# A spectral filter and an MLP mixed by a gate, in split fp32: another table of steps and another table of buffer slots

## The chip, the cores and the metric

The kernel runs on one core of one Trainium2 chip. The metric is the device time of one execution in microseconds (us); of several runs the median is taken. The engines are PE (TensorE: matmuls), PEld (its weight loads), DVE (VectorE), ACT (ScalarE), POOL (GpSimd) and SP (SyncE, which here issues DMAs).

## The reference: what is computed

The input x has 2048 rows (S) of 512 values (D), the MLP is 1792 wide (F).

```python
def _A_ref(x, w_r, w_i):
    X = rfft2(x) * (w_r + 1j * w_i)
    return irfft2(X, s=(S, D))
def _B_ref(x, w1, b1, w2, b2):
    return gelu(x @ w1 + b1) @ w2 + b2
g = sigmoid((x * gate_w).sum(-1, keepdims=True))
return g * a + (1 - g) * b
```

## The kernel before

**The work.** Branch A is the spectral filter. The two-dimensional FFT is done as matmuls with tables of cosines and sines. Per group of rows, a transform along D (`pd`, from the sums and differences eo and w that DVE builds of x) is copied to `zb` in halves and multiplied by `tf` (`py`); radix-4 butterflies over the 16 groups run on DVE (L665 to L673: b0s, b0d, y), the filter is multiplied in (m and wf, L765 to L769), and the butterflies run back. The inverse is `pz` (from the table tg, multiplied by the gate at L797, and pq), copied to `zb`, and `pa`. Of each pair of pa tiles, ACT copies one (od, L844), and DVE takes sum and difference with the other (u L854, v L855). L864 makes w of u and v, POOL adds the gate's part with an accumulating DMA (L867), and SP writes w out (L868).

Branch B is the MLP in 14 blocks of 128 of F. Per block f, `ph` holds x·W1 (512 columns wide), ACT does the gelu in place (L904), the result is split into g_fh and g_fl (ACT L466, DVE L467), and `po` (first pass, groups of rows 0 and 1) or `poB` (second pass) accumulates it times W2 over a range of blocks; the sums of ranges are put together in DRAM (`bacc`) by POOL's accumulating DMAs (L407). In the second pass a part of the x·W1 products is formed with fewer matmuls from sums of tiles (`nu`, `ux`, L1090 and on).

**The halves.** Every value is held as a high and a low half that PE takes as fp32r, and every product is three matmuls: high·high, low·high and high·low (suffixes h and l: mxh and mxl of x, wa0h and wa0l of W1's block 0, wb0h and wb0l of W2's block 0). A matmul is 128x512 unless a row says otherwise. For blocks of W2, and W1's later blocks, `halve` (L872) makes the halves: SP loads the block (L877, `..._raw`), ACT rounds it to the high half (L878), ACT writes the negative high half into the low half's tile (L472), and POOL issues a DMA that adds the block to it again (L407). W1's first blocks are loaded by SP (L890, L893; tile war) and split by ACT (L894) and DVE (L896). Block 0's and the first two groups of x come in two halves each (L503 by ACT's queue, L505 and L890 by SP's).

**What sets the order.** The kernel first records 2015 steps in a graph (`Graph.add`), each with an engine, the buffers it reads and writes, and a cost and a lag for a planner that ran beforehand. `Graph.schedule` then emits them in the order that the table ORDER (L125 to L204) gives by step numbers, and takes each buffer's slot in its pool from the table SLOTS (L206 to L225). Cost and lag are not read when the kernel is built. An engine runs its instructions in the order in which they are emitted, and waits at the first one whose inputs aren't there. So ORDER sets the queue of each engine, the DMA issues of SP, ACT and POOL among them, and SLOTS sets which earlier reader a buffer must wait for.

**The start and the end.** PE first runs fillers: six 128x512 matmuls of a zero tile and FILL = 10 of 128x256, tile `none` (L416). They keep it running until the first halves of x and W1 are there. At the end (`last`) the second pass's last poB tiles are subtracted from y on DVE (L1171) and written out by SP (L1174); of the last tile, the second 256 columns are computed apart (poB_33256), subtracted in two pieces (L1164) and written by SP and by ACT's queue (L1169).

Of the kernel before, what the change touches and what calls it, by code (L numbers as in the profile page):

```python
# [345 lines left out]
def tile_kernel(ctx: ExitStack, tc: tile.TileContext, xt, xc, w1, w2, b1, b2, x0g, wf, wrev, out, consts):  # L346
# [10 lines left out]
    vec, act, pe, sp = nc.vector, nc.scalar, nc.tensor, nc.sync  # L357
# [5 lines left out]
    add = g.add  # L363
# [517 lines left out]
    def load_w(n, f):  # L881
        first = n == "a" and f == 0
        h, l = W[n, f] = [buf("w", [P, D], F32R, f"w{n}{f}{k}", cls=n + k, parts=2 if first and k == "h" else 1) for k in "hl"]
        src = (w1 if n == "a" else w2)[f]
# [394 lines left out]
```

## Time and profile before

| | us |
|---|---|
| runs: lowest, median, highest | 365.43, 366.06, 366.5 |
| the profiled execution | 364.17 |
| its span | 362.3 |
| PE busy | 356.1 (98%) |
| DVE busy | 330.8 (91%) |
| ACT busy | 253.6 (70%) |
| POOL busy | 70.6 (19%) |
| first real matmul starts | 5.50 |
| last matmul starts | 358.23 |

The span runs from the first instruction of the profile to the last event; what the execution takes beyond it lies around it. The granted TensorE clock was full throughout. A matmul's record is longer than the distance to the next one's start, since matmuls overlap, so PE's progress is read from starts. In a row of a timeline stand the start, the duration, the engine, the line, the operation, output <- inputs, the shape and the number of instructions in the row; in brackets stands the idle time before it, and what ended it. fp32 matmuls (pd, pz) leave two records each.

### The profile page before, as it was taken

The page shows a single profiled execution, that of the slowest core. Times are in us where ns is not written, and L with a number is a line of the kernel's source. Part 1 is how long each engine was busy: PE and PEld are TensorE (multiplying, and loading weights), DVE is VectorE, ACT ScalarE, POOL GpSimd, SP SyncE. Part 2 cuts the span into 40 slices and gives each one's busy share as a digit, 9 for nine tenths or more (in the row PEclk, how much of TensorE's full clock was granted, in tenths as well). Part 3 has the DMA queues.
Part 4 walks back from the last instruction along what each step waited for, and adds up shares of the span by engine and source line. Part 5 has one row for each costly group of instructions (what it writes and reads, how often), then busy time and mean ns, then how long its engine had stood idle before and what let it go on. Part 6 is the DMA issues. An engine that isn't in the chain of part 4 may idle for free.

```text
span 362.3 us, 5722 instructions
## 1 busy us (share of the span) xinstructions
PE 356.1 (98%) x1808; PEld 302.2 (83%) x1808; DVE 330.8 (91%) x745; ACT 253.6 (70%) x471; POOL 70.6 (19%) x91
## 2 busy tenths in 40 slices
PE   8999999999999999999999999999999999999995
PEld 6988898898877888888888888888888888888885
DVE  5969999799978999999999999979989899899994
ACT  4984688789985563348468764899999986786100
POOL 1030000111021240111224300000432222003220
PEclk9999999999999999999999999999999999999999
DMA  7999597377689899897998954445686588858787
GB/s 242 369 337 263 176 322 203 102 162 184 208 147 237 199 261 211 198 342 226 217 263 152 148 113 134 103 133 166 83 146 123 85 149 208 166 164 203 168 228 221
DMA packets 46494, 70.34 MB, mean 194 GB/s; under 512 B 5376, under 2 KB 19200, under 8 KB 46464
## 3 DMA queue, kind: packets, MB, share of 16 engines
q1 hardware_dynamic: 34592, 48.93, 41.5%
q0 software_dynamic: 11440, 20.72, 37.1%
q10 hardware_dynamic: 432, 0.33, 0.3%
q8 instruction: 14, 0.23, 0.3%
q14 instruction: 16, 0.13, 0.1%
HBM read 48.32 MB, written 19.41 MB: 187 GB/s over the span
## 4 chain that ended last, share of the span: by engine, by line
PE 85%; DMA 5%; DVE 4%; ACT 3%; SPq 1%; issue 1%; DVEq 0%
PE poB L416 21%; PE po L416 20%; PE ph L416 14%; PE ux L1090 10%; PE nu L1090 8%; PE pz L416 4%; PE pd L416 3%; PE py L416 3%; PE pa L416 3%; DMA wb1l<-in_w 2%; DMA wb1l_raw<-in_w 2%; DMA y<-ownr 1%; ACT ph L904 1%; DVE b0s L665 0%; SPq L893 0%
## 5 line engine op out<-in xcount | busy, mean ns | idle before, releaser
L904 ACT ACTIVATE ph<-ph,b1t 128x512 f32<-128x512 f32 x28 | 18.4, 656 | 17.9 <-PE ph L416 17.8
L803 ACT ACTIVATE sw<-y,al 64x512 f32<-64x512 f32 x32 | 22.9, 721 | 1.2 <-DVE y L669 0.5
L407 POOL DMA_DIRECT2D bacc<-oB x16 | 13.9, 936 | 47.1 <-ACT oB L982 46.1
L407 POOL DMA_DIRECT2D bacc<-o x16 | 15.6, 977 | 35.8 <-ACT o L982 35.5
L765 DVE TENSOR_TENSOR m<-y,wf 128x514 f32<-128x514 f32 x32 | 21.3, 691 | 0.3
L982 ACT ACTIVATE o<-po 128x512 f32<-128x512 f32 x16 | 9.5, 596 | 15.4 <-PE po L416 9.9
L416 PEld LDWEIGHTS pz<-tg,pq 128*128 128x128 f32 x128 | 17.1, 191 | 1.9 <-PE pz L416 0.4
L416 PE MATMUL pz<-tg,pq 128*128 128x128 f32 x128 | 17.8, 275 | 0.3 <-DVE v L855 0.3
L416 PE MATMUL pd<-cf,w 128*128 128x129 f32 x128 | 17.7, 274 | 0.0
L1090 PE MATMUL nu<-xf,wa0h 128*128 128x512 f32 x56 | 17.4, 392 | 0.0
L416 PE MATMUL py<-zb,tf 128*128 128x258 f32 x96 | 17.3, 297 | 0.0
L416 PEld LDWEIGHTS pd<-cf,w 128*128 128x128 f32 x128 | 16.6, 190 | 0.6
L607 DVE TENSOR_TENSOR zb<-pd,zb 128x256 fp32r<-128x256 f32 x32 | 13.1, 419 | 4.1 <-ACT zb L604 2.2
L632 ACT ACTIVATE y<-pys 64x257 f32<-64x257 f32 x32 | 13.1, 417 | 3.5 <-DVE pys L629 3.0
L810 DVE SCALAR_TENSOR_TENSOR pq<-y,al,sw 128x256 f32<-128x256 f32 x32 | 14.9, 483 | 0.6 <-ACT sw L806 0.5
L416 PEld LDWEIGHTS pa<-zb,ci 128*128 128x128 f32 x96 | 13.7, 188 | 1.4
L416 PEld LDWEIGHTS py<-zb,tf 128*128 128x128 f32 x96 | 14.1, 190 | 0.9
L416 PE MATMUL pa<-zb,ci 128*128 128x256 f32 x96 | 14.3, 281 | 0.0
L822 ACT ACTIVATE zb<-pz 128x512 fp32r<-128x512 f32 x16 | 9.4, 597 | 6.5 <-PE pz L416 6.4
L604 ACT ACTIVATE zb<-pd 128x256 fp32r<-128x256 f32 x32 | 11.2, 387 | 3.5 <-PE py L416 2.2
L823 DVE TENSOR_TENSOR zb<-pz,zb 128x512 fp32r<-128x512 f32 x16 | 11.0, 691 | 2.8 <-ACT zb L822 2.8
L574 DVE TENSOR_TENSOR w<-eo 128x256 f32<-128x256 f32 x32 | 13.1, 421 | 0.3
(700 smaller groups left out, 1279.9 us busy)
## 6 DMA issues: line engine op xcount, KB each, us to landing
wf<-in_wf SPq DMA_DIRECT2D x16, 257.0 KB, 4.9
bacc<-o POOLq DMA_DIRECT2D x16, 256.0 KB, 7.0
bacc<-oB POOLq DMA_DIRECT2D x16, 256.0 KB, 4.2
xf<-in_xt SPq DMA_DIRECT2D x14, 256.0 KB, 4.9
wr<-in_w SPq DMA_DIRECT2D x14, 256.0 KB, 5.0
tf<-tf SPq DMA_DIRECT2D x16, 192.0 KB, 5.1
bacc<-o SPq DMA_DIRECT2D x8, 256.0 KB, 3.8
bacc<-oB SPq DMA_DIRECT2D x8, 256.0 KB, 2.2
```

The lines of the kernel that those rows point to most:

```text
L407: return add("pool", 2.3 * kb / 340, 3.4, lambda: nc.gpsimd.dma_start(dst(), src(), accum_op=ALU.add), reads, writes, rank)
L416: pe.matmul(ps, w, x, start=start, stop=stop)
L574: v(lambda s=s, op=op: vec.tensor_tensor(w.ap()[:, s], eo.ap()[:, :, 0], eo.ap()[:, :, 1], op=op), 256, [eo], [(w, s)], feed)
L604: a(lambda c=c: act.activation(segs(xh, c), both(c), AF.Copy), 256, [ps[c]], [(xh, c)], 0)
L607: v(lambda c=c: vec.tensor_tensor(segs(xl, c), both(c), segs(xh, c), op=ALU.subtract), 256, [ps[c], (xh, c)], [(xl, c)], 0)
L632: a(lambda o=o, i=i: act.activation(Y[j].ap()[o:o + HP, 1], pys.ap()[i:i + HP, 1], AF.Copy), 257, [(pys, 1)], [(Y[j], 1 + k)], 0, more=0.1)
L765: v(lambda mk=mk, k=k, y=y, w=w: vec.tensor_tensor(mk.ap(), y.ap(), w.ap()[:, k:k + 1, :ND].to_broadcast([P, 2, ND]), op=ALU.mult), 514, [ ...
L803: a(lambda sw=sw, y=y, o=o, i=i: act.activation(sw.ap()[o:o + HP], y.ap()[i:i + HP, ::-1, :HD], AF.Copy, scale=al.ap()[i:i + HP, 0:1]), 51 ...
L810: v(lambda sw=sw, pq_=pq_, y=y, j=j, k=k, op=op: vec.scalar_tensor_tensor(pq_.ap()[:, k], y.ap()[:, k, :HD], al.ap()[:, 1 + j:2 + j], sw.a ...
L823: v(lambda n=n, ps=ps: vec.tensor_tensor(zl.ap()[:, :, :, n], ps.ap(), zh.ap()[:, :, :, n], op=ALU.subtract), 512, [ps, (zh, n)], [(zl, n) ...
L904: a(lambda: act.activation(ps.ap(), ps.ap(), AF.Gelu_apprx_tanh, bias=b1t.ap()[:, f:f + 1]), 600, [b1t], [ps]).table = "gelu"
L1090: pe.matmul(o.ap(), w(wi, e), FX[j].ap()[:, xi, e], start=first, stop=k == 5, skip_group_check=not start)
```

## The change

The tables ORDER and SLOTS are replaced, and three of the planner's lags are changed: for the two halves of x's group 0 (L503), of group 4 (L505) and of W1's block 0 (L890). The graph is the same: the same 2015 steps with the same dependencies, so each engine runs the same instructions, in another order and with other slots. A tile's number changes with the order (zb_101 and zb_128 are zb_86 and zb_107 in the new order).

The diff has 103 replaced lines of the two tables; the first of ORDER and the last of SLOTS stand here, and all the rest:

```diff
 ORDER = """
-13 0 2 3 4 5 6 7 8 9 10 11 12 15 38 14 16 26 25 506 508 18 507 527 109 1 37 39 27 19 64 17 511 23 554 543 530 167 509
...
+0 2 15 3 22 13 1 16 23 24 38 37 508 509 14 4 5 6 7 26 27 506 507 25 527 39 65 17 18 19 64 66 543 61 511 8 9 10 109 515
...
@@ -500,9 +500,9 @@
     x4 = buf("w", [P, NQ, P], F32, "xf4", parts=2, cls="x")
     XF = {0: x0, 4: x4}
     for k in range(2):
-        add("act", 0.4, 3.0, lambda k=k: act.dma_start(x0.ap()[:, 2 * k:2 * k + 2].rearrange("p a b -> p (a b)"),
+        add("act", 0.4, 2.4 + 0.35 * k, lambda k=k: act.dma_start(x0.ap()[:, 2 * k:2 * k + 2].rearrange("p a b -> p (a b)"),
                                                        x0g[:, k * HD:(k + 1) * HD]), [], [(x0, k)], 0)
-        add("sp", 128 / 340, 2.4, lambda k=k: sp.dma_start(x4.ap()[:, 2 * k:2 * k + 2], xt[4][:, 2 * k:2 * k + 2]), [], [(x4, k)],
+        add("sp", 128 / 340, 1.5 + 0.05 * k, lambda k=k: sp.dma_start(x4.ap()[:, 2 * k:2 * k + 2], xt[4][:, 2 * k:2 * k + 2]), [], [(x4, k)],
             0.01 + 0.01 * k)
     for j in NORD[2:4]:
         XF[j] = load_x(j, "f")
@@ -887,7 +887,7 @@
         if first:
             for k in range(2):
                 o = slice(k * HD, (k + 1) * HD)
-                add("sp", 128 / 340, 1.4 + 0.2 * k, lambda o=o: sp.dma_start(t.ap()[:, o], src[:, o]), [], [(t, k)])
+                add("sp", 128 / 340, 1.0 + 0.25 * k, lambda o=o: sp.dma_start(t.ap()[:, o], src[:, o]), [], [(t, k)])
                 v(lambda o=o: vec.tensor_copy(h.ap()[:, o], t.ap()[:, o]), 256, [(t, k)], [(h, k)])
         elif own:
             dma(lambda: sp.dma_start(t.ap(), src), 256, [], [t])
```

Where the order changes, three places.

The first is ACT's queue in the first 25 us, in two cuts. ph is x·W1 before the gelu, wb the blocks of W2, L878 a high half, L472 the negative high half that POOL's accumulation waits for. Around wb1l, before:

```order
L904 ACTIVATE ph_0_160<-ph_0_160,b1t 128x512
L878 ACTIVATE wb4h<-wb4l_raw 128x512
L559 ACTIVATE mxh_240<-xf_136 128x512
L904 ACTIVATE ph_1_192<-ph_1_192,b1t 128x512
L472 ACTIVATE wb4l<-wb4h 128x512
L466 ACTIVATE g_1h<-ph_1_192 128x512
L894 ACTIVATE wa4h<-war_143 128x512
L878 ACTIVATE wb2h<-wb2l_raw 128x512
L472 ACTIVATE wb2l<-wb2h 128x512
L472 ACTIVATE wb1l<-wb1h 128x512
```

and in the new order:

```order
L878 ACTIVATE wb0h<-wb0l_raw 128x512
L472 ACTIVATE wb0l<-wb0h 128x512
L878 ACTIVATE wb1h<-wb1l_raw 128x512
L904 ACTIVATE ph_1_170<-ph_1_170,b1t 128x512
L466 ACTIVATE g_1h<-ph_1_170 128x512
L904 ACTIVATE ph_0_137<-ph_0_137,b1t 128x512
L894 ACTIVATE wa3h<-war_165 128x512
L466 ACTIVATE g_0h<-ph_0_137 128x512
L894 ACTIVATE wa4h<-war_159 128x512
L472 ACTIVATE wb1l<-wb1h 128x512
```

wb1l's L472 stood 23rd in ACT's queue, behind the two instructions each of wb4 and wb2; now it stands 19th, ahead of them. Around wb3l, before (zb are the copies of PE's pd tiles):

```order
L878 ACTIVATE wb3h<-wb3l_raw 128x512
L904 ACTIVATE ph_4_318<-ph_4_318,b1t 128x512
L466 ACTIVATE g_4h<-ph_4_318 128x512
L472 ACTIVATE wb3l<-wb3h 128x512
L604 ACTIVATE zb_101<-pd_386 128x256
L604 ACTIVATE zb_128<-pd_363 128x2x128
```

and in the new order:

```order
L466 ACTIVATE g_3h<-ph_3_268 128x512
L604 ACTIVATE zb_86<-pd_349 128x2x128
L604 ACTIVATE zb_107<-pd_353 128x2x128
L878 ACTIVATE wb3h<-wb3l_raw 128x512
L604 ACTIVATE zb_107<-pd_357 128x256
L904 ACTIVATE ph_4_302<-ph_4_302,b1t 128x512
L604 ACTIVATE zb_86<-pd_359 128x256
L472 ACTIVATE wb3l<-wb3h 128x512
```

wb3l's L472 stood 32nd, ahead of all copies of pd; now it is 35th, behind four of them and behind the gelu of block 4. POOL issues the accumulations in the order wb0l, wb1l, wb2l, wb3l, wb4l in both, so wb4l's waits behind wb3l's in both, too.

The second place is DVE's queue around g_9l, the low half of the gelu's output of block 9. b0s, b0d, y, m and wf belong to the filter. Before:

```order
L667 TENSOR_TENSOR b0d_1528<-y 128x514
L667 TENSOR_TENSOR y<-b0s_1524,b0s_1500 128x514
L665 TENSOR_TENSOR y<-b0d_1517,b0d_1528 128x2x257
L765 TENSOR_TENSOR m_8_1545<-y,wf_1344 128x514
L765 TENSOR_TENSOR m_8_1548<-y,wf_1344 128x514
L667 TENSOR_TENSOR y<-b0d_1528,b0d_1517 128x2x257
L767 TENSOR_TENSOR y<-m_8_1548,m_8_1545 128x257
L769 TENSOR_TENSOR y<-m_8_1548,m_8_1545 128x257
L665 TENSOR_TENSOR y<-b0s_1500,b0s_1524 128x514
L467 TENSOR_TENSOR g_9l<-ph_9_1502,g_9h 128x512
```

and in the new order:

```order
L665 TENSOR_TENSOR b0s_1521<-y 128x514
L665 TENSOR_TENSOR b0s_1526<-y 128x514
L667 TENSOR_TENSOR b0d_1529<-y 128x514
L667 TENSOR_TENSOR b0d_1531<-y 128x514
L665 TENSOR_TENSOR y<-b0s_1526,b0s_1521 128x514
L765 TENSOR_TENSOR m_0_1548<-y,wf_1175 128x514
L765 TENSOR_TENSOR m_0_1567<-y,wf_1175 128x514
L665 TENSOR_TENSOR y<-b0d_1531,b0d_1529 128x2x257
L467 TENSOR_TENSOR g_9l<-ph_9_1505,g_9h 128x512
L667 TENSOR_TENSOR y<-b0s_1521,b0s_1526 128x514
L467 TENSOR_TENSOR g_8l<-ph_8_1480,g_8h 128x512
```

g_9l stands behind eight instructions of the filter in place of ten. On PE, the first matmul that reads block 9's output came 24 matmuls behind the last ph of that block, and in the new order 39 matmuls behind it.

The third place is the end of SP's queue, the writes of the output. Before:

```order
L1174 DMA out<-oB_31_4142 128x512
L1174 DMA out<-oB_23_4148 128x512
L868 DMA out<-w_4085 128x2x256
L1174 DMA out<-oB_30_4160 128x512
L868 DMA out<-w_4109 128x2x256
L1174 DMA out<-oB_32_4168 128x512
L1174 DMA out<-oB_33_4187 128x256
L1169 DMA out<-oB_33_4187 128x128
```

and in the new order:

```order
L1174 DMA out<-oB_23_4126 128x512
L1174 DMA out<-oB_30_4150 128x512
L1174 DMA out<-oB_33_4166 128x256
L868 DMA out<-w_4112 128x2x256
L1174 DMA out<-oB_31_4178 128x512
L1174 DMA out<-oB_32_4191 128x512
L1169 DMA out<-oB_33_4166 128x128
```

oB_32's 256 KB moved behind oB_33's first part, the last w and oB_31. On PE the 12 matmuls of poB_32 with 512 columns, which stood ahead of both parts of poB_33, now stand between them.

Beyond these, at the start SP issues the halves of x's group 4 and of W1's block 0 in turn (x, W1, x, W1) where it issued both of x first, two of the ten fillers follow the first products in place of standing ahead of them, DVE makes one eo in place of two ahead of wa0l, and the last memset of zb (L516) stands ahead of POOL's accumulations in place of behind the first five.

190 rows, old and new, of tables (ORDER, SLOTS) are left out of this document.

## The prediction

> **What bounds the kernel now.** I read the page's shares first, then the chain, then what PE waited for, then PE's timeline at the places where its starts are further apart than usual.
>
> ```profile
> span 362.3 us, 5722 instructions
> PE 356.1 (98%) x1808; PEld 302.2 (83%) x1808; DVE 330.8 (91%) x745; ACT 253.6 (70%) x471; POOL 70.6 (19%) x91
> PE 85%; DMA 5%; DVE 4%; ACT 3%; SPq 1%; issue 1%; DVEq 0%
> ```
>
> PE carries 85% of the chain, and the 98% leave 6 us without a matmul, most of them before the first product and after the last. The profiled execution took 364.17 us: its span of 362.3 and 1.87 around it. The median of the runs is 366.06, which is 1.89 more; I work out the difference against the profiled execution and carry it over to the median unchanged. The new tables keep every step, so PE's own work (the number, kinds and shapes of its matmuls) is the same, and the order can only move the time in which PE has nothing to start. That is little. After the first products the view of PE's waits names only two that last over 0.1 us, one for DVE's v (L855) and this one (total, times, longest):
>
> ```profile
> PE po L416 <- DMA wb1l<-in_w: 0.2, 1, 0.2
> ```
>
> The modelled end of a matmul hides part of such a wait, so I measure each by the distance of starts. PE's timeline around the second block of the MLP:
>
> ```profile
> 22.96 0.48 PE L416 MATMUL po<-g_0h,wb0h 128*128 128x512 f32 x1
> ...
> 25.09 0.39 PE L416 MATMUL po<-g_1h,wb1h 128*128 128x512 f32 x1
> 25.32 0.39 PE L416 MATMUL po<-g_1l,wb1h 128*128 128x512 f32 x1
> 25.89 0.50 PE L416 MATMUL po<-g_1h,wb1l 128*128 128x512 f32 x1 [0.18 <-DMA wb1l<-in_w]
> 26.23 0.40 PE L416 MATMUL po<-g_1h,wb1h 128*128 128x512 f32 x1
> ```
>
> Undisturbed, 512-wide matmuls start 0.23 us apart (25.09, 25.32). Here the next two follow after 0.57 and 0.34: the wait named as 0.2 really costs 0.34 + 0.11 = 0.45 us.
>
> **Term 1, wb1l: −0.45.** The low half of a W2 block is made by ACT (L472, the negative high half) and then an accumulating DMA that POOL issues (L407). ACT, POOL, and the issue-to-landing times of wb0l, wb1l and wb2l in that order:
>
> ```profile
> 17.67 0.61 ACT L472 ACTIVATE wb1l<-wb1h 128x512 fp32r<-128x512 f32 x1
> 22.64 0.62 ACT L472 ACTIVATE wb3l<-wb3h 128x512 fp32r<-128x512 f32 x1
> 23.24 0.94 ACT L604 ACTIVATE zb<-pd 128x256 fp32r<-128x256 f32 x3
> ```
>
> ```profile
> 18.58 0.86 POOL L407 DMA_DIRECT2D wb1l<-in_w  x1 [4.51 <-ACT wb1l L472]
> 19.14 1.19 POOL L407 DMA_DIRECT2D wb2l<-in_w  x1
> 23.56 0.85 POOL L407 DMA_DIRECT2D wb3l<-in_w  x1 [3.23 <-ACT wb3l L472]
> ```
>
> ```profile
> DMA to landing us min/median/max: 5.5/5.5/5.5
> DMA to landing us min/median/max: 7.3/7.3/7.3
> DMA to landing us min/median/max: 8.8/8.8/8.8
> ```
>
> 18.58 + 7.3 = 25.9, just when PE goes on. In the new order wb1l's ACT instruction stands four places earlier: wb4's two, wb2's two and an mxh now follow it, and one g_0h has come ahead. At 0.5 to 0.6 us each (17.67 0.61) that is 2.0 to 2.4 us, so POOL issues it near 16.4, and with 7.3 it lands at 23.7, with 8.8, the worst of the three, at 25.2. PE asks for it 11 matmuls of 0.23 behind the first po, at 25.5. The whole 0.45 goes, with 0.3 us left at the worst.
>
> **Term 2, g_9l: −0.4.** PE and DVE at 116.7:
>
> ```profile
> 116.89 0.39 PE L416 MATMUL po<-g_9h,wb9h 128*128 128x512 f32 x1
> 117.42 0.50 PE L416 MATMUL po<-g_9l,wb9h 128*128 128x512 f32 x1
> 117.75 0.40 PE L416 MATMUL po<-g_9h,wb9l 128*128 128x512 f32 x1
> ```
>
> ```profile
> 116.68 0.69 DVE L467 TENSOR_TENSOR g_9l<-ph,g_9h 128x512 fp32r<-128x512 f32 x1
> ```
>
> The starts lie 0.53 and 0.33 apart in place of 0.23: 0.40 us, because g_9l stood behind ten filter instructions on DVE. In the new order DVE has about the same queue ahead of g_9l, but PE puts 39 matmuls of 512 between block 9's last ph and its first po, where 24 stood: 15 × 0.23 = 3.4 us more room, over eight times the wait, so it goes.
>
> **Term 3, two groups of the inverse transform: −0.5 and −0.3.** PE at 320 and 264, and the first and last rows of a stretch at 273 (pa x4, pz x4, pa x4, pz x4 start between them):
>
> ```profile
> 264.34 0.60 PE L416 MATMUL pz<-tg,pq 128*128 128x128 f32 x4
> 264.70 0.48 PE L416 MATMUL poB<-g_5h,wb5hb 128*128 128x512 f32 x1
> 265.01 0.40 PE L416 MATMUL poB<-g_5l,wb5hb 128*128 128x512 f32 x1
> ...
> 273.45 0.62 PE L416 MATMUL pa<-zb,ci 128*128 128x256 f32 x4
> 275.51 0.73 PE L1090 MATMUL nu<-xf,wa0h 128*128 128x512 f32 x2
> ...
> 319.72 0.60 PE L416 MATMUL pz<-tg,pq 128*128 128x128 f32 x4
> 320.60 0.57 PE L416 MATMUL pz<-tg,pq 128*128 128x128 f32 x3 [0.27 <-DVE v L855]
> ```
>
> ```profile
> 318.77 0.69 DVE L854 TENSOR_TENSOR u<-pa,od 128x512 f32<-128x512 f32 x1
> 319.76 0.69 DVE L855 TENSOR_TENSOR v<-pa,od 128x512 f32<-128x512 f32 x1
> ```
>
> Four pz records undisturbed take 0.36 (264.34 to 264.70), and the matmul behind them starts the next one 0.08 late (0.31 to 265.01). From 319.72 to 320.60 it is 0.88: 0.5 us lost, waiting for v, the last reader of the pa tile whose PSUM slot pz takes. v ran late because DVE had other work ahead of u. In the new order DVE has u, one pq and v behind a 512-wide ACT copy of the other pa tile: 0.61 as for wb1l, and 1.68 from u's start to v's end, 2.3 us. PE has 12 wide matmuls at 0.23 and a whole pz group of 0.88 between that pa tile and the pz that takes the slot, 3.6 us. So the wait goes, unless DVE comes to u over 1.3 late. The 2.06 us from 273.45 to 275.51 compare with 2 × 0.36 + 0.08 + 8 × 0.12 (256-wide matmuls start 0.12 apart, 358.11 to 358.23 below) = 1.76: 0.3 lost in a group of pz wedged between pa groups. The new order has a similar wedge, with the pz whole and not in halves; I take the 0.3 as gained, and its return is in the first rival.
>
> **Term 4, the start: −0.1.**
>
> ```profile
> 6.56 0.76 DVE L571 TENSOR_TENSOR eo<-xf 128x256 f32<-128x256 f32 x2
> 7.23 0.69 DVE L896 TENSOR_TENSOR wa0l<-war,wa0h 128x512 fp32r<-128x512 f32 x1
> ```
>
> ```profile
> 7.97 0.73 PE L416 MATMUL ph<-mxh,wa0l 128*128 128x256 f32 x4 [0.46 <-DVE wa0l L896]
> ```
>
> SP now issues the first half of block 0's weights second in place of third, and DVE does one eo (half of 0.76) ahead of wa0l in place of two. So wa0l comes 0.38 us earlier, and PE gains that; two of the ten filler matmuls then run behind this group, at 0.12 to 0.2 each, so 0.1 is left. Bounds: −0.4 if the fillers fall into a wait, +0.3 if the x tile's half, now third, is the later.
>
> **Term 5, what is late next: wb3l, +0.6.** The price of the better wb1l is paid by wb3l. In the order of before its ACT instruction runs ahead of the copies that wait for PE (22.64, then zb at 23.24). In the new order it stands behind four zb copies and a gelu, and the third of these copies needs the last pd of this batch, so it can't start before about 23.2. From there: a copy 0.3 (three take 0.94), the gelu some 0.6 like the other 512-wide ones, a copy 0.3, wb3l itself 0.62: ACT ends near 25.0, and POOL issues near 25.3 (0.3 behind, as 22.64 + 0.62 against 23.56), 1.7 later than before. PE asks for wb3l near 32.0: 29 po at 0.23, four pd groups of 0.44 and 6 py at 0.12 lie ahead of it, 9.1 us, behind the first po at 22.9. The lead is 6.7 us. With the 7.3 of wb1l it would stall 0.6; with the 5.5 of wb0l, which was issued alone, nothing; with the 8.8 of wb2l 2.1. POOL issues wb4l right behind wb3l, as wb2l behind wb1l, so wb1l's row is the nearest: I take 0.6 and keep 0 to 2.1. wb4l itself is asked for 4 us later and has room. A stall is likeliest here of all places in the new order.
>
> By the Trainium skill, "DMA: Bandwidth & Descriptors", section "Anatomy of one DMA — SWDGE (gpsimd) path", a DMA issued from GpSimd takes about 2.0 us plus its bytes at 436 GB/s: an estimate of 2.6 us for these 256 KB, and no stall, so the sum would be 0.6 lower. The rows above say 5.5 to 8.8 for an accumulating one beside other traffic, and the 25.89 row bears them out; I go by the rows.
>
> **Term 6, the end: +0.2.**
>
> ```profile
> 356.92 0.97 SPq L1174 DMA_DIRECT2D out<-oB  x2
> 358.87 0.33 SPq L1169 DMA_DIRECT2D out<-oB  x1
> ```
>
> ```profile
> 358.11 0.28 PE L416 MATMUL poB<-g_13l,wb13hb 128*128 128x256 f32 x1
> 358.23 0.28 PE L416 MATMUL poB<-g_13h,wb13lb 128*128 128x256 f32 x1
> ```
>
> The two DMAs of 356.92 carry 256 KB (oB_32) and 128 KB (oB_33's first part). The new order computes oB_33's first part ahead of oB_32, and so oB_32's last matmul stands 12 matmuls of 0.12 ahead of the end and not 24. Its 256 KB are therefore issued about 1.2 us later, near the last matmul's start. The span now ends 4.07 us behind that start (362.3 − 358.23), and the final pieces are still issued 0.64 behind it (358.87). What is late is 128 KB more than before, and the last slices of the page's row of GB/s show what moves:
>
> ```profile
> GB/s 242 369 337 263 176 322 203 102 162 184 208 147 237 199 261 211 198 342 226 217 263 152 148 113 134 103 133 166 83 146 123 85 149 208 166 164 203 168 228 221
> ```
>
> At 221 GB/s they take 0.6 us, at the 369 of the busiest slice 0.35, and nothing where they fit beside the final pieces: 0 to 0.6, I take 0.2. The accumulation of the last inverse tile stands ahead of oB_31, oB_32 and the final piece in SP's queue: if it lands late, all three wait, by up to the 3.3 us that lie between the quickest and the slowest accumulation above; that price is close to the collision's below and is held by the same end of the range.
>
> **Nothing:** the three lags at L503, L505 and L890 are numbers for the planner; nothing that is issued reads them. For other moves I count +0.1: several tiles have a shorter lead than before, none so short that its rows force a stall.
>
> **The sum:** −0.45 − 0.4 − 0.5 − 0.3 − 0.1 + 0.6 + 0.2 + 0.1 = −0.85 us: 363.3 for a profiled execution, 365.2 as a median.
>
> **Rivals.** *The waits only move.* wb3l stalls for over 0.6, up to 2.1, or new stalls of 0.1 to 0.5 at pz, py and g tiles pay back the 1.75 of the first four terms. For it: DVE has 330.8 us of work in a span of 362.3, so a gain for one DVE instruction is a loss for another. Against: by the distance of starts PE's stalls after 13 us sum to under 3 us, so most of this order's exchanges already cost nothing. Time: 365.2 + 0.3 to 365.2 + 1.75, in the middle 366.2.
>
> *Slower: the earlier accumulations collide with loads.* The busy share of the DMA engines in 40 slices of 9.06 us:
>
> ```profile
> DMA  7999597377689899897998954445686588858787
> ```
>
> In slices 2 to 4 they are 90% busy and more. wb1l now comes near 16.4, 2.1 us earlier, into the loads of weights, x and tables on which ph_3, ph_4 and the first pd wait. wb2l, issued 0.56 behind wb1l, took 3.3 us longer to land than wb0l, which came alone (8.8 and 5.5). If the same 3.3 falls on a load with 1 us of lead, PE stalls 2.3 and the gains turn: 365.2 + 2.3 = 367.5. It decides once a load that PE needs by 25 us lands over 0.85 us later than it is asked for. Against it: the loads are issued from SP, and in the trace of before PE waits for no load by SP after 8 us.
>
> *It does nothing* (365.7 to 366.4): the numbers changed for the planner alone can do nothing, but the tables do change every queue, so this is only possible by chance and belongs to the first rival.
>
> By the same row, more may come out in ordinary runs: they take 1.89 more than the profiled one, and if part of that is late transfers, an order chosen on more draws of them might lose less (363.7).
>
> **How the numbers follow.** A run of this kernel can be told from no change at about 0.3%, 1.1 us; the forecast, 0.85, is below that. The forecast (364.4 to 366.0) has 0.45: its third below 364.96 is faster, 0.15, the rest, 0.30, is no difference. The first rival has 0.17, all within. The collision has 0.20, all slower. More than forecast, by the ordinary runs or by a wb3l that lands in time, has 0.18, faster. So 0.33 faster, 0.47 the same, 0.20 slower. The range takes in the better case down to 363.5 and reaches to 367.4, about the collision's middle; it leaves out the other half of the collision and a gain of over 2.5.
>
> **What would show it.** After 13 us PE's timeline has no gap at wb1l (near 25.4), none at the first po of block 9, and none over 0.1 where pz takes a pa tile's slot. POOL's wb1l row stands near 16, wb3l's near 25. PE's wait for wb3l is named, at 32, with about 0.6. The last matmul starts 1.05 earlier, near 357.2, and the span ends about 4.3 behind it. I am wrong if PE waits for an x, wa, cf or tf load between 13 and 30 us, if a wait over 0.5 appears elsewhere, or if the last matmul comes earlier and the span's end doesn't.

## The result, and the profile after

| | before | changed |
|---|---|---|
| runs (22 each): lowest, median, highest, us | 363.49, 365.96, 368.93 | 363.35, 365.42, 367.2 |
| the shown profiled execution, us | 364.17 | 365.96 |
| its span, us | 362.3 | 364.1 |
| first real matmul starts | 5.50 | 7.04 |
| first 128x512 product starts | 13.07 | 16.34 |
| last matmul starts | 358.23 | 360.16 |
| from there to the end of the span | 4.07 | 3.94 |

The ratio of the changed kernel to the one before is 0.9994, with a 95% interval of 0.9974 to 1.0013: 0.2 us less, between 0.95 less and 0.5 more (the two medians themselves lie 0.54 apart). That is no difference that can be told from none. (Three executions of the experiments took 398.9 to 924.58 us, the profiled one of e4 among them at a granted clock of 0.655, and no row and no median below uses them.)

The two shown executions say something else: the changed one is 1.8 us longer. The table splits this into three stretches. The start lost 16.34 − 13.07 = 3.27. From there to the last matmul it is 343.82 in place of 345.16, a gain of 1.34. The end gained 0.13. All three matter below. First the page of the changed kernel, its span, busy times and chain:

```profile
span 364.1 us, 5722 instructions
PE 358.0 (98%) x1808; PEld 305.1 (84%) x1808; DVE 330.0 (91%) x745; ACT 254.1 (70%) x471; POOL 70.3 (19%) x91
PE 97%; DMA 1%; SPq 0%; DVE 0%; issue 0%; DVEq 0%
```

PE has 97% of the chain, where it had 85%: past the start hardly anything but PE sets the end. The view of PE's waits names these two alone:

```profile
PE ph L416 <- DVE wa0h L891: 1.3, 1, 1.3
PE none L416 <- DVE zero L484: 1.1, 1, 1.1
```

The second is the wait ahead of the fillers; the first is new. PE's timeline there, from the last ten fillers on:

```profile
2.93 2.76 PE L416 MATMUL none<-zero 128*128 128x512 f32 x10
7.04 1.94 PE L416 MATMUL ph<-mxh,wa0h 128*128 128x128 f32 x8 [1.35 <-DVE wa0h L891]
...
11.02 1.05 PE L416 MATMUL ph<-mxh,wa1h 128*128 128x256 f32 x4
11.87 1.05 PE L416 MATMUL ph<-mxl,wa1h 128*128 128x256 f32 x4
...
13.94 0.64 PE L416 MATMUL ph<-mxh,wa1h 128*128 128x256 f32 x4
14.42 0.64 PE L416 MATMUL ph<-mxl,wa1h 128*128 128x256 f32 x4
```

The reader is to see two things. PE has nothing to do for 1.35 us ahead of its first product. And four 256-wide products take 0.85 us near 11 (0.21 each) and 0.48 near 14 (0.12 each): until 13.4 PE runs at half its pace. It had not been faster before, either: the ten fillers, two of 128x512 and eight of 128x256, take 2.76, where 0.23 and 0.12 each would make 1.4. SP's DMA queue and DVE in the same stretch:

```profile
1.19 0.41 SPq L890 DMA_DIRECT2D war<-in_w  x1
1.65 0.43 SPq L505 DMA_DIRECT2D xf<-in_xt  x1
2.12 0.43 SPq L890 DMA_DIRECT2D war<-in_w  x1
```

```profile
4.13 0.29 DVE L891 CAST wa0h<-war 128x256 fp32r<-128x256 f32 x1 [0.31 <-DMA war<-in_w]
6.60 0.29 DVE L891 CAST wa0h<-war 128x256 fp32r<-128x256 f32 x1 [2.17 <-DMA war<-in_w]
```

The two L890 rows are the two halves of W1's block 0, and by the table's step numbers (508 ahead of 506) the one issued at 1.19 is the **second** half. The first half, which PE's first product reads, is issued fourth, at 2.12. Its cast runs at 6.60, and PE starts when it is nearly done. The same two views of the shown execution of before, where the two L890 go out one behind the other, first half first:

```profile
1.64 0.92 SPq L890 DMA_DIRECT2D war<-in_w  x2
```

```profile
4.95 0.29 DVE L891 CAST wa0h<-war 128x256 fp32r<-128x256 f32 x1 [0.38 <-DMA war<-in_w]
```

The places that the prediction named, in the changed kernel. POOL, the issue-to-landing times of wb1l and wb3l, and PE where it asks for them:

```profile
19.79 0.87 POOL L407 DMA_DIRECT2D wb1l<-in_w  x1 [7.54 <-ACT wb1l L472]
...
28.55 0.85 POOL L407 DMA_DIRECT2D wb3l<-in_w  x1 [4.37 <-ACT wb3l L472]
```

```profile
DMA to landing us min/median/max: 6.0/6.0/6.0
DMA to landing us min/median/max: 4.0/4.0/4.0
```

```profile
28.59 0.39 PE L416 MATMUL po<-g_1l,wb1h 128*128 128x512 f32 x1
28.82 0.39 PE L416 MATMUL po<-g_1h,wb1l 128*128 128x512 f32 x1
29.05 0.39 PE L416 MATMUL po<-g_1h,wb1h 128*128 128x512 f32 x1
...
35.24 0.39 PE L416 MATMUL po<-g_3l,wb3h 128*128 128x512 f32 x1
35.47 0.39 PE L416 MATMUL po<-g_3h,wb3l 128*128 128x512 f32 x1
```

Starts 0.23 apart at wb1l and at wb3l: no stall at either. (POOL's two rows were forecast near 16.4 and 25.3; both stand some 3.3 later, which is the 3.27 of the start.) The group of pz behind the wide products at 321, on PE:

```profile
321.74 1.50 PE L416 MATMUL pz<-tg,pq 128*128 128x128 f32 x12
322.99 0.48 PE L416 MATMUL poB<-g_8h,wb8hb 128*128 128x512 f32 x1
```

Twelve pz records pass in 1.25 us with no gap inside. And the end, PE and SP's queue:

```profile
360.16 0.28 PE L416 MATMUL poB<-g_13h,wb13lb 128*128 128x256 f32 x1
```

```profile
358.42 1.74 SPq L1174 DMA_DIRECT2D out<-oB  x2
360.99 0.33 SPq L1169 DMA_DIRECT2D out<-oB  x1
```

### The profile page after: what moved, and what is told of

Its sections match the earlier page's. It is cut to its first block, busy times and chain, and to the rows that moved or that the text cites. A ratio compares the mean times of both kernels' runs of the same rounds, so it can differ in the third digit from the quotient of the medians.

```text
span 364.1 us, 5722 instructions
## 1 busy us (share of the span) xinstructions
PE 358.0 (98%) x1808; PEld 305.1 (84%) x1808; DVE 330.0 (91%) x745; ACT 254.1 (70%) x471; POOL 70.3 (19%) x91
## 4 chain that ended last, share of the span: by engine, by line
PE 97%; DMA 1%; SPq 0%; DVE 0%; issue 0%; DVEq 0%
PE ph L416 22%; PE poB L416 21%; PE po L416 21%; PE ux L1090 10%; PE nu L1090 8%; PE pd L416 4%; PE pz L416 4%; PE py L416 3%; PE pa L416 3%; DMA war<-in_w 1%; SPq L505 0%; PE pown L416 0%; PE none L416 0%; SPq L890 0%; DVE wa0h L891 0%
## 5 line engine op out<-in xcount | busy, mean ns | idle before, releaser
L632 ACT ACTIVATE y<-pys 64x257 f32<-64x257 f32 x32 | 13.4, 418 | 6.4 <-DVE pys L629 5.7
L571 DVE TENSOR_TENSOR eo<-xf 128x256 f32<-128x256 f32 x32 | 12.9, 419 | 0.0
L604 ACT ACTIVATE zb<-pd 128x256 fp32r<-128x256 f32 x32 | 12.0, 382 | 1.1 <-PE pd L416 0.5
```

The source lines that it names most:

```text
L571: v(lambda s=s, op=op: vec.tensor_tensor(eo.ap()[:, s], x.ap()[:, 0:2], x.ap()[:, 2:4], op=op), 256, [x], [(eo, s)], feed)
L604: a(lambda c=c: act.activation(segs(xh, c), both(c), AF.Copy), 256, [ps[c]], [(xh, c)], 0)
L632: a(lambda o=o, i=i: act.activation(Y[j].ap()[o:o + HP, 1], pys.ap()[i:i + HP, 1], AF.Copy), 257, [(pys, 1)], [(Y[j], 1 + k)], 0, more=0.1)
```

## The experiments

Two things were to be told apart. Either the new order gains about 1.3 us behind the start and its own start, with the halves of W1's block 0 exchanged, gives it back; or the shown execution of before was an early one, and both kernels start late in most executions. The runs of each call share the runs of the kernel before, taken beside them (medians 365.44 for e1 to e4, 365.67 for e5 to e8, 366.47 for e9 to e11, 366.13 for e12).

### Both kernels again (e1, e2, e5)

No edit: e1 is the kernel before, e2 and e5 the changed one, e5 with timed rounds.

> The kernel before, unchanged, looked at once more. Two theories on why 1.3 us of waits disappeared behind the start and the median moved only 0.2. Theory A (the start is the order's): the new order lets PE's first product wait for the fourth DMA of SP's queue, the order of before for the third, so the new start is later in every execution. Theory B (the start is the draw's): how early the first loads land differs from execution to execution, whatever the order, and the profile of before was a lucky one. A expects the first product at 5.3 to 5.8 us and the first 128x512 product at 12.9 to 13.4, as in the profile shown (5.50 and 13.07). B expects another start here, the first product anywhere from 5.3 to 7, the first 128x512 product up to 16.

> The changed kernel, unchanged, looked at once more. Theory A expects its late start again: first product at 6.7 to 7.3 us, first 128x512 product at 15.5 to 16.5 (7.04 and 16.34 in the profile shown). Theory B expects a start that is not tied to this order, the first product as early as 5.3 in some execution. Both expect the waits at wb1l, g_9l and at the pz behind v to stay away.

> The changed kernel, unchanged, timed beside the next three and seen in a third execution. Theory A (its start is later than that of before, since the first product waits for the fourth DMA): a ratio of 0.998 to 1.000, 1 us above the two kernels with other starts (0.996 and 0.995). Theory B (the starts differ by the draw, and the gain is the 1.0 to 1.3 us between the first 128x512 product and the last): a ratio of 0.996 to 0.997, as these two.

| | e1, before | e2, changed |
|---|---|---|
| one execution, us | 366.46 | 365.01 |
| first real matmul | 6.71 | 6.72 |
| first 128x512 product | 15.68 | 15.39 |
| from there to the last matmul | 344.85 | 343.86 |
| from there to the end | 4.07 | 3.85 |

e5 took 365.51 (362.4 to 367.09), ratio 0.9987 (0.9957 to 1.0016). In e1 the kernel before starts its wide products 2.6 us later than in its shown execution, and as late as the changed one. PE in e1:

```profile
6.71 0.41 PE L416 MATMUL ph<-mxh,wa0h 128*128 128x128 f32 x2 [0.59 <-DVE wa0h L891]
...
10.08 1.05 PE L416 MATMUL ph<-mxh,wa1h 128*128 128x256 f32 x4
```

It too waits for the first half, and runs at half pace behind that. SP issues that half at 1.64 or 1.65 in all four profiles of the old order, and its cast runs at 4.95 in the shown one, at 6.27, 6.39 and 6.44 in e1, e8 and e10; with the changed kernel's queue, where it goes out at 2.12, the cast runs at 6.60 (shown), 6.29, 6.62 and 6.38 (e2, e5, e6). So the execution on which the prediction was built was an early one (364.17, where the 22 runs go from 363.49 to 368.93), as theory B has it. Theory A isn't refuted by that: e5's ratio lies where A put it (0.998 to 1.000) and above B's 0.996 to 0.997, and none of the changed kernel's three profiles has an early start. The gain behind the start holds in either case: 344.85 − 343.86 = 0.99 here.

### SP's order of the first four loads (e3, e4, e11)

e3 exchanges the two halves of W1's block 0 in the new table, the casts with them; e4 and e11 (one kernel, twice) put both halves behind x's, first half first.

```diff
-0 2 15 3 22 13 1 16 23 24 38 37 508 509 14 4 5 6 7 26 27 506 507 25 527 39
+0 2 15 3 22 13 1 16 23 24 38 37 506 507 14 4 5 6 7 26 27 508 509 25 527 39
```

```diff
-0 2 15 3 22 13 1 16 23 24 38 37 508 509 14 4 5 6 7 26 27 506 507 25 527 39
+0 2 15 3 22 13 1 14 23 24 38 37 16 506 507 4 5 6 7 26 27 508 509 25 527 39
```

> The changed kernel with only the two halves of W1's block 0 exchanged in the queues of SP and DVE: the half that PE's first product reads is the second of SP's DMAs in place of the fourth, the other half the fourth. Theory A: the first product starts with the end of the fillers, near 5.3 us, PE does not fall idle ahead of it, and the time is 1.0 us under the changed kernel's: a ratio of 0.997 to the kernel before. Theory B: nothing in the median, a ratio of 0.9994 as the changed kernel's.

> The changed kernel with SP's first four DMAs in the order of the kernel before: both halves of x's group 4, then the first and the second half of W1's block 0; the casts on DVE in that order too. All else is the new order's. Theory A: the start of the kernel before comes back, the first product waits for the third DMA, and the inner gain of 1.3 us shows: a ratio of 0.9965 to the kernel before. Theory B: as the changed kernel, 0.9994.

> The changed kernel with SP's first four DMAs in the order of before and 6 wide fillers, as e4 but seen undisturbed. If the order of SP's first four DMAs is worth 1 us and more (theory A): 0.995 to 0.996 again, first product at 5.9 to 6.3, 128x512 near 14.2. If the 0.995 was chance: 0.998, as the changed kernel, first product and 128x512 as there (6.7 to 7.05 and 15.1 to 16.3).

e3: 364.75, ratio 0.9962 (0.9935 to 0.9989). e4: 363.73, 0.995 (0.9921 to 0.9978). e11: 364.85, 0.9951 (0.9918 to 0.9985). All three stand below the changed kernel's 0.9994 and 0.9987, but the intervals meet. PE in e3:

```profile
5.49 0.41 PE L416 MATMUL ph<-mxh,wa0h 128*128 128x128 f32 x2
7.51 0.89 PE L416 MATMUL ph<-mxh,wa0h 128*128 128x128 f32 x6 [1.60 <-DVE wa0h L891]
```

The first product starts 1.2 to 1.6 us earlier than in e2 and in the shown execution, and then PE waits 1.60 for the other half: the wide products start at 16.01. The exchange moves the wait from the first product to the third. e11's ratio is the one expected of an order that is worth 1 us, but its profile isn't: the first product starts at 6.48 and the wide ones at 15.56. Whether SP's order alone moves the median stays open.

### A start without a gap (e6, e7, e8)

Six more of the wide fillers, in the changed kernel (e6), in e4's kernel (e7) and in the kernel before (e8). They fill the time that PE idles ahead of its first product, and delay that product where its operands come early; no other queue changes.

```diff
     def warm():
-        for _ in range(6):
+        for _ in range(12):
```

> The changed kernel with 12 in place of 6 wide fillers ahead of the first product, 1.36 us more at 0.227, so that PE is not idle between 5.3 and 6.6 us. Theory C (the idle stretch ahead of the first product makes PE run the 256-wide products at half pace some 2 us later, 0.21 in place of 0.12 each, for 3 to 4 us): no half pace after 8 us, the first 128x512 product near 13.8 in place of 15.4, the time 1.5 us under the changed kernel's. Theory D (the half pace comes from something else, the loads for instance): half pace stays, no gain, and 0 to 1 us lost in executions whose loads land early.

> The changed kernel with SP's first four DMAs in the order of before, and 12 in place of 6 wide fillers. Theory C: 1.5 us under the same kernel with 6 (ratio 0.995 there): 0.991. Theory D: 0.995 to 0.998.

> The kernel before with 12 in place of 6 wide fillers. Theory C: the half pace that its second profile shows (0.21 for a 256-wide product from 9.3 to 12.6) goes here, too, whatever the order: a ratio of 0.996. Theory D: 1.000 to 1.003.

| | median (range), us | ratio to before | first product | first 128x512 | from there to the last matmul |
|---|---|---|---|---|---|
| e6 | 363.5 (362.82 to 363.91) | 0.9936 (0.9911 to 0.9961) | 7.20 | 14.01 | 343.66 |
| e7 | 363.15 (362.82 to 363.56) | 0.9933 (0.9906 to 0.9961) | 7.15 | 13.56 | 343.72 |
| e8 | 365.02 (363.56 to 365.72) | 0.9973 (0.9945 to 1.0001) | 6.83 | 14.40 | 344.74 |

The fillers themselves run at half pace at first, the wide ones 0.43 us apart, so six more cost up to 2.6 us and not the 1.36 that was forecast. e6 starts its first product 0.48 **later** than e2 and its wide products 1.38 **earlier**. The view by stretches of e2, and then of e6 (the length, then busy us and instructions of PE, PEld, DVE, ACT and POOL, then the granted clock, DMA share, GB/s):

```profile
5.30:6.70 1.40, 0.29 (x2) 0.10 (x2) 0.41 (x2) 0.42 (x1) 0.00 (x0) 1.00 0.95 342
6.70:8.80 2.10, 1.84 (x13) 1.52 (x13) 2.10 (x5) 1.80 (x3) 0.00 (x0) 0.99 1.06 391
8.80:12.50 3.70, 3.70 (x18) 3.70 (x19) 3.67 (x8) 2.59 (x5) 0.90 (x1) 0.54 1.05 397
```

```profile
5.30:6.70 1.40, 1.40 (x7) 1.17 (x7) 0.32 (x2) 0.17 (x1) 0.00 (x0) 1.00 0.82 300
...
8.80:12.50 3.70, 3.63 (x30) 3.63 (x31) 3.67 (x9) 2.80 (x5) 0.90 (x1) 1.00 1.06 394
```

From 8.80 to 12.50 PE is busy throughout in both, but it does 18 matmuls in e2 and 30 in e6: the granted clock is 0.54 and 1.00. PE in e2, and in e6:

```profile
10.22 1.05 PE L416 MATMUL ph<-mxh,wa1h 128*128 128x256 f32 x4
11.07 1.05 PE L416 MATMUL ph<-mxl,wa1h 128*128 128x256 f32 x4
```

```profile
9.69 0.64 PE L416 MATMUL ph<-mxh,wa1h 128*128 128x256 f32 x4
10.17 0.64 PE L416 MATMUL ph<-mxl,wa1h 128*128 128x256 f32 x4
...
14.01 0.40 PE L416 MATMUL ph<-mxh,wa2h 128*128 128x512 f32 x1
```

So the idle stretch costs twice: 1.1 us of waiting, and some 2 us behind it by the clock (6.72 to 15.39 is 8.67 in e2, 7.20 to 14.01 is 6.81 in e6). The second is the larger part, and fillers take it away. e6 gains 2.0 us of median against e5 in the same call, and its executions lie within 1.1 us where e5's spread over 4.7. The ratios of e7 and e8 lie between what the theories C and D expected; it is the half pace, gone from the products of all three profiles, that decides for C. The runs don't separate two things that more fillers do: they close the idle stretch, and they give PE time to come to its full pace ahead of the first product (by the starts near 6.2 in e6), which it hadn't done in the changed kernel's shown execution.

e6 against e8 is the change itself with the start covered in both: 363.5 − 365.02 = −1.5 us. The profiles split it into −0.39 at the start, −1.08 behind it, −0.13 at the end. This is the gain of the new tables that the plain comparison doesn't show. e6 against e7 is SP's order with the start covered: 0.35 us of median, with ranges that overlap, and 14.01 against 13.56 in the profiles.

### Which fillers are needed (e9, e12)

e9 is e7 with ten wide fillers, and with the two narrow ones (steps 11 and 12) that stood between real products moved ahead of the first. e12 is e9 with eight.

```diff
-511 8 9 10 109 515 516 517 518 519 510 520 110 11 565 530 33 554 528 12 534
+511 8 9 10 11 12 109 515 516 517 518 519 510 520 110 565 530 33 554 528 534
...
-        for _ in range(12):
+        for _ in range(10):
```

> The best so far (the changed kernel with SP's first four DMAs in the order of before and 12 wide fillers) with 10 wide fillers, and with the two narrow ones that stand between products moved ahead, so that all 10 narrow ones stand there: the fillers end 0.45 - 0.24 = 0.2 us earlier, near 6.9, and no filler stands between products. Theory C (an idle stretch brings the half pace, fillers as such cost only their time): first product near 6.9, first 128x512 product near 13.1 in place of 13.56, 0.45 us less: a ratio of 0.992. If executions whose loads land at 7 fall back to the half pace, their spread widens from 0.7 to 2 us and the ratio is 0.993 to 0.996.

> e9 with 8 wide fillers in place of 10. The fillers end 0.45 us earlier, near 6.5 to 6.7. Where the halves of W1's block 0 have landed by then, as in the profile of e9 (cast at 5.4), the first product starts 0.45 earlier and so does the end: 362.4. Where they land at 6.3 and later, as in six of the other profiles, PE is idle for some 0.5 us and theory C says that a part of the half pace comes back: 363 to 364, and a spread of over 1 us. I expect a median of 362.6 with a wider spread than the 0.7 of e9.

e9: 362.86 (362.57 to 363.28; five runs), ratio 0.9896 (0.9877 to 0.9916), the quickest of all, 1.0% below the kernel before in the same call (against e7, which is from another call, 0.29 us less, too little to show what its own step is worth); the changed kernel wasn't timed in that call, but its own ratio and this one's (0.9974 to 1.0013 and 0.9877 to 0.9916) are far apart. Its wide products start at 13.35. e12: 363.48 (362.81 to 364.16), 0.9935 (0.9908 to 0.9962), 0.9 us above the expected median, with the wider spread that was expected. Eight still keep the clock at 1.00 from 5 to 13 us, and the first product starts at 6.38, 0.81 earlier than in e9; but the wide ones start at 13.62, because PE then waits 0.32 for mxl and 0.20 for wa0l. The first product was not the limit of the start: DVE's work on the halves was, and in e12 it also begins later, since the second of the two casts waits for its DMA until 6.25 (in e9 both run from 5.44). So it isn't shown that eight are fewer than needed. e12's profile shows one more thing, PE at 122:

```profile
122.30 0.39 PE L416 MATMUL po<-g_6h,wb6l 128*128 128x512 f32 x1
123.40 0.50 PE L416 MATMUL po<-g_5h,wb5h 128*128 128x512 f32 x1 [0.71 <-ACT o L982]
```

Here 1.10 lies between two starts in place of 0.23: ACT's copy of a po tile came late, in this one profile of the new order, at a place where the starts of the other eight are 0.34 apart at most. ACT had stood 2.79 us for a DMA (bacc<-o) until 119.54, where the others stand 1.0 to 1.9. So a lead of the new order can be thin, and one execution of nine paid for it.

### One exchange on DVE in the old order (e10)

e8's kernel with u and v (steps 1470 and 1471) right behind ACT's od (1467); v goes ahead of one y and one pq among others.

```diff
-1494 1858 1467 1213 1615 1658 1470 1489 1912 1499 1887 1816 1471 1473
+1494 1858 1467 1470 1471 1213 1615 1658 1489 1912 1499 1887 1816 1473
```

> The kernel before with 12 wide fillers, and on DVE u and v of the third inverse tile moved ahead of one y and one pq: v ends about 0.7 us earlier, the pq that the same pz needs 0.6 later. It does one part of term 3 alone. If v is what that pz waits for, the gap of 0.25 to 0.5 us ahead of it (near 321 us) goes and the last product starts 0.25 to 0.5 earlier than in the kernel before with 12 fillers (344.74 us behind the first 128x512 one): 344.3 to 344.5; ratio 0.996 where 0.9973 stood. If the wait is on pq or on ACT's copy as well, the gap stays or moves to the earlier pz, and the distance is 344.7 again.

364.45 (364.0 to 365.25), ratio 0.994 (0.9921 to 0.996). PE in e8, and in e10:

```profile
320.78 1.82 PE L416 MATMUL pz<-tg,pq 128*128 128x128 f32 x12
322.36 0.70 PE L1090 MATMUL ux<-xft,wath 128*128 128x512 f32 x2
```

```profile
320.43 1.50 PE L416 MATMUL pz<-tg,pq 128*128 128x128 f32 x12
321.69 0.71 PE L1090 MATMUL ux<-xft,wath 128*128 128x512 f32 x2
```

The group takes 1.26 in place of 1.58. From the first wide product to the last matmul e10 needs 343.97, e8 344.74: 0.77 less, more than the 0.25 to 0.5 expected. Both have the same matmuls in the same order, so the difference can be followed start by start: 0.32 goes in this group, 0.18 ahead of the pz group before it and 0.10 within that one (0.46 to 0.36), together 0.60, by two DVE instructions that changed places. Another 0.11 is e8's wait at g_9l, near 118, which the exchange doesn't touch, and the rest is scattered. The 0.60 is over half of the 1.0 to 1.1 that the new tables gain there.

## Why the prediction was right, and where it was not

**The result** (365.2 forecast, 365.42 measured, no difference forecast and found) came out by the forecast of a small gain. For the profiled execution it forecast 363.3, and that one took 365.96. The step that fails is the base: I took the shown execution of before as typical and added 1.89 to reach the median. That difference is the start: in e1 it is 2.61 us later (15.68 against 13.07), and the rest of e1 is 0.3 shorter. That the median came out within 0.2 of the forecast is luck in part: against a typical execution Terms 1 and 2 had nothing to gain, the start cost about 1 us more than forecast, and the prices of Terms 5 and 6 didn't fall due, which about cancel.

**Behind the start** the forecast was −0.95 (Terms 1, 2, 3, 5 and the +0.1). Measured are −1.34 between the shown profiles, −0.99 between e1 and e2, −1.08 between e8 and e6. The size is right, the terms are only partly so:

- *Terms 1 and 2* (wb1l, g_9l): gone in the changed kernel, as forecast, but they belonged to the shown execution. In e1 POOL issues wb1l at 20.76, it takes 7.2, and PE asks for it at 28.17: a lead of 7.4 where the shown execution had 7.0, and no wait. e1 has none at g_9l either, e8 one of 0.11. Against these executions the two terms are worth 0 to 0.11.
- *Term 3* (pz): right, and most of the gain: it stands in all three executions of the old order. In e1 and e8 the groups at 320 lose 0.53 + 0.31 and 0.18 + 0.32, and the wedge at 273 takes 2.08 and 2.06 against the same 1.76; in the changed kernel eight pz records stand there whole and pass in 0.81, undisturbed. e10 shows that the order of u and v on DVE is the cause at 320 for 0.60 us. It need not be the only one: the 0.53 of e1 is named as a wait of 0.37 for ACT's od, not for v.
- *Term 5* (wb3l, +0.6): the lead was right, 35.47 − 28.55 = 6.9 against 6.7. The price was wrong: it landed in 4.0, and in 3.9 to 4.8 in the other executions of the new order, not in 7.3. In the 4 us from its issue the core's DMA engines moved 304 GB/s in the shown execution of before and 88 in the changed kernel's; over all profiles it is 239 to 315 with landings of 5.2 to 7.3 us in the old order, and 82 to 192 with 3.9 to 4.8 in the new. That fewer transfers ran beside it is the likely reason; no run varied it alone. By the Trainium skill, "DMA: Bandwidth & Descriptors", section "Anatomy of one DMA — SWDGE (gpsimd) path", the estimate is 2.6 us; the runs lie above that everywhere, but here nearer to it than to the row I chose.

**Term 4** (the start, −0.1) is the step that failed outright. It says that SP now issues "the first half of block 0's weights second in place of third"; the second half goes second and the first half fourth, which the step numbers of the table told and the names in a queue's rows don't. In the shown execution PE's first wait of 1.35 is for that half. The place in the queue is not all of it, since e3's exchange only moves the wait and the old order's half comes about as late in three of four profiles. The prediction also took when the loads land from one execution, and priced a wait at the start by its own length, where the half pace makes it about 3 us in all (e2). Of 22 and 22 runs the medians differ by 0.2 us by their ratio, while the stretch behind the start and the end gain 1.1 to 1.5 in every pair of profiles. So the start of the changed kernel must be about 1 us later in the median; this is worked out from those, not seen, since the start of the wide products scatters from 13.07 to 15.68 in single profiles of before and from 15.10 to 16.34 in those of the changed kernel. What makes it later, SP's order or something else at the start, stays open.

**Term 6** (the end, +0.2): oB_32 goes out late as forecast, in the row of 358.42, yet the span ends 3.94 and 3.85 behind the last matmul's start and not 4.3. The final piece, issued at 360.99, sets the end, and the 256 KB ahead of it cost nothing that shows.

**Rivals.** No load collided: PE waits for none between 13 and 30 us in any profile of the new order. New stalls did not pay back the gain, but for e12's one of 0.87. What paid the gain back lies ahead of the stretch that the first rival looked at.

## What to carry to other kernels

Read a start by several executions before an order is chosen or judged by one: here the same kernel starts its wide matmuls at 13.07 or at 15.68. And read PE's pace by the distance of starts, beside the clock's record. When PE waits for its first operands, keep it busy until they land with room for the slower executions: ten wide fillers and SP's old order give 362.86 where the changed kernel alone has 365.42 (in different calls; by their ratios 1.0% and 0.1% below before). Where a table's rows carry the same names for two halves, follow the numbers of the steps.

## What the runs showed of the hardware

PE starts at half pace in every profile, and the clock's record doesn't show it. The record reads 1.00 from the first filler on, in the execution before as well, but wide fillers start 0.43 us apart where wide products later start 0.23 apart. By the starts PE comes to its full pace while the fillers run at 4.4 us in the earliest case (e5) and 6.7 in the latest (e9); in the shown execution of before it has done so by 5.02, from where narrow fillers start 0.12 apart. In the changed kernel's shown execution it is still at half pace when the fillers end, and stays there until 13.4, all under a record of 1.00: there the distance of starts tells it, and the record doesn't.

An idle stretch of 1 to 2 us ahead of and between the first products can halve the clock again, and not at once. In e2 PE is idle for most of 5.30 to 6.70, runs at a granted 0.99 from 6.70 to 8.80, and then at 0.54 until 12.50. In all five executions with six fillers that show it in the clock's records (e1, e2, e3, e5, e11), the mean granted clock from 5 to 13 us is 0.79; at half clock that is (1 − 0.79) × 8 / 0.5 = 3.4 us. PE's named waits there sum to 1.29 to 1.94 us. In the shown execution of before and in the filled ones (e6 to e10, e12) they sum to 0.76 at most, and the clock is 1.00. The timed runs say the same by their mean granted clocks: 0.998 to 1.0 in all 56 runs of the filled kernels, 0.994 or 0.995 in 9 of e5's 12.

By the Trainium skill, "TensorE: Matmul & The Clock Gate", section "Part 1: The HAM clock gate (the "warmup" mystery)", the clock falls to a half after an idle window of about 3.4 us, and the window runs freely. The traces of those five agree with the half and with 3.4 us as the length; e2 differs in the cause, since PE was busy there for 0.29 of the 1.40 us and for 1.84 of the 2.10 behind them, and the clock fell all the same.
